# Marks in bfloat16 and a slot table entered from exactly split values: an FFT, mixture-of-experts and SoLU kernel on one core

## The chip, the cores and the metric

The kernel runs on one core of a Trainium2 chip. The metric is the device time of one execution in microseconds (us). Every time below is of the kernel before; lines such as L553 are lines of its source.

## The reference, cut to what matters

```python
def reference(**kw):
    y = _attn_ref(x, w_r, w_i, b_r, b_i)      # 8 x 3072 x 256: FFT over 3072, complex 256x256 mix, shrink, inverse FFT
    y = _moe_ref(y.reshape(24576, 256), w_gate, w1, w2, capacity)
    return _moe2_ref(y, w_in, w_out, g_ln)    # 256 -> 1024, SoLU, layer norm, 1024 -> 256

def _moe_ref(x, w_gate, w1, w2, capacity):    # 8 experts, capacity 768 here
    logits = x @ w_gate
    expert_idx = np.argmax(logits, axis=1)
    ...                                       # gate_w: softmax probability of the chosen expert
    for i in range(N):                        # in token order: the first `capacity` tokens of an expert keep a slot
        e = expert_idx[i]
        if counts[e] < capacity:
            disp[e, counts[e]] = x[i]
            pos[i] = counts[e]; counts[e] += 1; keep[i] = True
    h = np.maximum(np.einsum('ecd,edf->ecf', disp, w1), 0.0)
    y = np.einsum('ecf,efd->ecd', h, w2)
    ...                                       # out[i] = gate_w[i] * y[expert_idx[i], pos[i]] where kept, else 0
```

## The kernel before

The sequence of 3072 is handled as 96 x 32 per batch. For each of the first three batches a first stage (`forward`) is followed by twelve units (`units`): stage 2 of the FFT for unit u+1 (L393, with L396 to L399 behind it), the mix of unit u (L426, with L432, L434 and L435 behind it), the first inverse stage of unit u-1 (L443), and then whatever `middle(u)` hands in. A `tail` turns the batch back (L475, L480, L298, L491), and in it `route` works out which expert and which slot each token gets.

Only three batches are needed for every expert's capacity to be filled with these inputs; the rest is under a runtime condition. After them sixteen blocks of 384 slots run (`run_blocks`): two blocks for each of eight experts, with up projection (L798, L801, L802), down projection (L815 to L818), the 256 to 1024 projection (L842 to L845), SoLU and norm, and the last projection (L913). All the fp32 products of the experts are made from a high and a low part; `split` (L271) lets ScalarE copy the high part (L272) and another engine subtract to get the low part (L273).

The route of a batch has three parts. `local` finds the expert and the weight's numerator. `place` finds each token's slot, as `lo` (slot modulo 128) and `hi` (slot divided by 128). Nine steps then enter the tokens into a table `tab` of 128 x 2 x 48: for each slot the token's number plus one and its weight. The 32 tokens of a partition are taken in eight chunks of four. `mark(c)` makes for a chunk two tables of ones and zeros on VectorE, `rows` (where `lo` equals a column, 4 x 128, L553) and `hit` (where `hi` equals a column, 4 x 48, L554), and GpSimd multiplies `hit` by the token numbers and by the weights (L556, two instructions a chunk). `enter(c)` multiplies `rows` by the products on TensorE (L562: four fp32 matmuls of 96 columns, each shown as two instructions) and VectorE adds the result to `tab` (L564). There are two buffers for the chunks.

The order on each engine is fixed when the program is built, and every engine takes its queue in order. The nine steps of batch 0's route are handed in by `middle` in units 0 to 8 of batch 1, those of batch 1's route in batch 2, and those of batch 2's route in block 0, at the letters R of `ORDER_0`. `all_places` (L588) follows the last one and makes the indices by which later blocks gather. In block 0 the letters E hand in the steps of the second expert's weights (`expert_steps`, eight splits of 128 x 512, L272 and L273), which block 1 is the first to use.

Of the kernel before, what the change touches and what calls it, by code (L numbers as in the profile page):

```python
# [12 lines left out]
BF16 = mybir.dt.bfloat16  # L13
U16 = mybir.dt.uint16
ACTF = mybir.ActivationFunctionType
ALU = mybir.AluOpType
AX = mybir.AxisListType

NB, S, N1, N2, D = 8, 3072, 96, 32, 256
# [34 lines left out]
EARLY = (0, 1)  # L54
# [72 lines left out]
def _body(tc, x, w_r, w_i, b_r, b_i, w_gate, w1, w2, w_in, w_out, g_ln, cap, con, out):  # L127
# [4 lines left out]
    ncol = nslot // 128  # L132
    assert ncol <= 128
    mm = nc.tensor.matmul
# [8 lines left out]
    with sp as sb, dp as dr, pp as ps:  # L143
# [17 lines left out]
        def v(o, n, p=128):  # L161
            k, o = o >> 20, o & 0xFFFFF
            return tiles[k][:p, o : o + n]

        def v3(o, a, b, p=128):
            return v(o, a * b, p).rearrange("p (a b) -> p a b", a=a)

        def v4(o, a, b, c, p=128):
            return v(o, a * b * c, p).rearrange("p (a b c) -> p a b c", a=a, b=b)
# [327 lines left out]
        def route(tok_src, chunk_buffers):  # L497


            rt = [v(o_rt + 256 * i, 256, N1) for i in (0, 1, 2, 3, 4, 0)]  # L500
            sm = [v(o_rt + 1312 + 32 * i, 32, N1) for i in range(8)]
            ne = lambda a: a.rearrange("p (n e) -> p n e", e=NE)
            en = lambda a: a.rearrange("p (e n) -> p n e", e=NE)
            bc = lambda a: a.rearrange("p (n o) -> p n o", o=1).to_broadcast([N1, N2, NE])
            be = lambda a: a.rearrange("p (o e) -> p o e", o=1).to_broadcast([N1, N2, NE])
            tok, lo, hi, weight = v(o_rt + 1280, 32, N1), sm[4], sm[5], sm[1]
            tot2 = sm[3][:, 0:NE]

            def local():
                pool.dma_start(out=tok, in_=tok_src)  # L510
                vec.tensor_reduce(sm[0], lg, AX.X, ALU.max)
                vec.tensor_tensor(ne(rt[0]), lg, bc(sm[0]), ALU.subtract)
                act(rt[1], rt[0], ACTF.Exp)
                vec.tensor_scalar(rt[2], rt[0], 0.0, None, ALU.is_ge)
                vec.tensor_tensor(ne(rt[2]), ne(rt[2]), be(w8), ALU.mult)
                vec.tensor_reduce(sm[2], ne(rt[2]), AX.X, ALU.max)
                vec.tensor_tensor(en(rt[3]), ne(rt[2]), bc(sm[2]), ALU.is_equal)
                vec.tensor_tensor_scan(rt[4], seg, rt[3], 0.0, ALU.mult, ALU.add)
                tot = rt[4].rearrange("p (e n) -> p e n", e=NE)[:, :, N2 - 1 : N2].rearrange("p e o -> p (e o)")
                vec.tensor_copy(tot2, tot)  # L520

            def place():
                p = psum("pso")
                mm(p[:N1, 0:NE], low, tot2, start=True, stop=False)
                mm(p[:N1, 0:NE], one, tsum, start=False, stop=True)
                vec.tensor_tensor(sm[4][:, 0:NE], p[:N1, 0:NE], ecap, ALU.add)
                vec.tensor_tensor(tsum, tsum, tot2, ALU.add)
                vec.tensor_tensor(en(rt[4]), en(rt[4]), be(sm[4][:, 0:NE]), ALU.add)
                vec.tensor_tensor(en(rt[5]), en(rt[4]), be(lim), ALU.is_gt)
                vec.scalar_tensor_tensor(rt[4], rt[5], float(FAR), rt[4], ALU.mult, ALU.add)  # L530
                vec.tensor_tensor(rt[3], rt[3], rt[4], ALU.mult)
                vec.tensor_reduce(sm[5], en(rt[3]), AX.X, ALU.add)
                slot, row = sm[6].bitcast(I32), sm[7].bitcast(I32)
                vec.tensor_copy(slot, sm[5])
                vec.tensor_scalar(row, slot, 127, None, ALU.bitwise_and)
                vec.tensor_scalar(slot, slot, 7, None, ALU.logical_shift_right)
                vec.tensor_copy(lo, row)
                vec.tensor_copy(hi, slot)
                vec.tensor_reduce(weight, ne(rt[1]), AX.X, ALU.add)
                vec.tensor_scalar(weight, weight, 1e-9, None, ALU.add)  # L540
                vec.reciprocal(weight, weight)

            w = N2 // NCH
            wide = lambda a, c, m: a[:, w * c : w * c + w].rearrange("p (n o) -> p n o", o=1).to_broadcast([N1, w, m])
            same = lambda m: iota[:, 0:m].rearrange("p (o m) -> p o m", o=1).to_broadcast([N1, w, m])

            def views(c):
                o = chunk_buffers[c % len(chunk_buffers)]
                return v3(o, w, 128, N1), v4(o + 128 * w, w, 2, ncol, N1), v3(o + (128 + 2 * ncol) * w, w, ncol, N1)

            def mark(c):
                rows, cols, hit = views(c)
                vec.tensor_tensor(rows, same(128), wide(lo, c, 128), ALU.is_equal)  # L553
                vec.tensor_tensor(hit, same(ncol), wide(hi, c, ncol), ALU.is_equal)  # L554
                for i, a in enumerate((tok, weight)):
                    pool.tensor_tensor(cols[:, :, i], hit, wide(a, c, ncol), ALU.mult)  # L556

            def enter(c):
                rows, cols, _ = views(c)
                p = psum("psr")  # L560
                for j in range(w):
                    mm(p[:, 0 : 2 * ncol], rows[:, j], cols[:, j].rearrange("p a c -> p (a c)"), start=j == 0, stop=j == w - 1)  # L562
                t = tab.rearrange("p a c -> p (a c)")
                vec.tensor_tensor(t, t, p[:, 0 : 2 * ncol], ALU.add)  # L564

            steps = [lambda: mark(0)]
            for c in range(1, NCH):
                steps.append(lambda c=c: (mark(c), enter(c - 1)) if len(chunk_buffers) > 1 else (enter(c - 1), mark(c)))
            steps.append(lambda: enter(NCH - 1))
            return local, place, steps  # L570

# [612 lines left out]
        for b in range(FIRST):  # L1184
            last = b + 1 == FIRST
            steps = []

            def middle(u, b=b, last=last, marks=marks, steps=steps):
                if u == 0:
                    renew(o_hn)  # L1190
                    second[:] = second_steps()
                    steps.extend(step for chunk in second[3 * b : 3 * b + 3] for step in chunk)
                if b > 0 and marks:
                    marks.pop(0)()
                    if b == 2 and not marks:
                        early_places()
                zeros(ZEROS[b][u % 4])
                with pinned():
                    for _ in range(STEPS[b]):
                        if steps:  # L1200
                            steps.pop(0)()
                if not last and u in (4, 5, 6, 10, 11):
                    load_x(x[b + 1], {4: 0, 5: 1, 6: 2, 10: 3, 11: 4}[u])
                if last and u == 6:
                    renew(o_g)
                if last and GATHER <= u < GATHER + 2:
                    blocks[u - GATHER].gather()
                if last and u >= 6 and early:
                    early.pop(0)()
                    if early:  # L1210
                        early.pop(0)()

            def before_last(b=b, last=last, steps=steps):
                while steps:
                    steps.pop(0)()
                renew(o_hn)
                if last:
                    renew(o_ga)
                    blocks[0].transposes()
                    sums.extend(column_sums())  # L1220
                    sums.pop(0)()
                else:
                    begin(x[b + 1])

            units(middle, before_last)
            while sums:
                sums.pop(0)()
            renew(o_tt)
            if last:
                renew(o_wi2, o_hn)  # L1230
                second_half[0] = o_wi2
            if not last:
                forward(x[b + 1], begun=True)
                relays()
            else:
                renew(*o_q, o_wsb)
                side[0] = expert_steps(EARLY[1], slot_b, vec)
                side[0].pop(0)()
                side[0][LATER:LATER] = last_steps()
            local, place, marks = route(con["c_tok"][b], (o_hn + 1536, o_rt))  # L1240
            steps = {-at: [f] for f, at in zip((local, place), ROUTE[b])}
            if last:
                steps.setdefault(COUNT, []).insert(0, lambda: counts(cnt))
            tail(yview(ydram[b * S : (b + 1) * S, :]), steps)
# [81 lines left out]
```

## Time and profile before

| | |
|---|---|
| Time, median of 3 runs | 889.87 us (888.95 to 889.9) |
| The profiled execution | 889.02 us |
| Its span on the core | 887.4 us |
| TensorE, VectorE, ScalarE, GpSimd busy | 96%, 70%, 46%, 34% of the span |
| Mean granted TensorE clock | 0.985 |

PE is TensorE's matmuls, PEld its weight loads, DVE is VectorE, ACT ScalarE, POOL GpSimd. In the chain of work that ended last, each piece has its start, its length, and what it was. In a table by windows each row is a stretch (from:to in us), its length, then each engine's busy time with its count of instructions in brackets, the granted clock of TensorE as a share of full speed, the mean busy share of the DMA engines and GB/s. A row of a group of instructions has line, engine, operation, tiles, shapes and count, then busy us in total and the mean ns of one, then the idle time ahead of it. A row of a timeline has start, length, engine, line, operation. Instructions of one engine overlap at their ends, so the busy time of a stretch is less than the sum of durations.

### The profile page before, as it was taken

How to read it: one execution, taken by the hardware profiler on the slowest of the kernel's cores; microseconds unless marked ns; L12 is line 12 of the kernel's file. 1: busy time of each engine (PE TensorE's matmuls, PEld its weight loads, DVE VectorE, ACT ScalarE, POOL GpSimd, SP SyncE). 2: the span in 40 equal slices, each digit the busy share in tenths (PEclk: the TensorE clock that was granted, in tenths of full speed). 3: DMA queues.
4: the chain of work that ended last, by engine and by line, in shares of the span. 5: the costliest groups of instructions: out<-in, count | busy, mean ns of one | idle time of the engine just before them, and what ended most of it. 6: DMA issues, size and time to landing. Idle time of an engine off the chain costs nothing.

```text
span 887.4 us, 15851 instructions
## 1 busy us (share of the span) xinstructions
PE 851.6 (96%) x5884; PEld 734.1 (83%) x5884; DVE 621.4 (70%) x1434; ACT 410.4 (46%) x648; POOL 299.6 (34%) x463
## 2 busy tenths in 40 slices
PE   9799999999999989999999999999999999999993
PEld 3799459964799659988999889989889989999983
DVE  2376468745788568867787877868777778776771
ACT  2253344434444335444555545545555555544450
POOL 0000012100123024355564454445545545444343
PEclk9799999999999989999999999999999999999997
DMA  8989758996699143146376345355355354233120
GB/s 237 303 237 287 248 182 244 308 284 189 198 298 276 47 128 100 46 78 109 101 167 132 96 119 139 91 116 126 95 125 126 98 123 106 55 78 88 33 60 28
DMA packets 208683, 130.92 MB, mean 148 GB/s; under 512 B 123238, under 2 KB 190934, under 8 KB 208470
## 3 DMA queue, kind: packets, MB, share of 16 engines
q1 hardware_dynamic: 203894, 117.20, 50.3%
q0 software_dynamic: 4704, 12.63, 4.4%
q8 instruction: 48, 0.79, 0.4%
q14 instruction: 37, 0.30, 0.1%
HBM read 50.37 MB, written 50.33 MB: 113 GB/s over the span
## 4 chain that ended last, share of the span: by engine, by line
PE 86%; DMA 6%; DVE 4%; ACT 1%; issue 1%; POOL 0%; SPq 0%; DVEq 0%; ACTq 0%
PE psH L798 14%; PE pso L913 12%; PE psm L426 12%; DMA r<-r 5%; PE psY L818 5%; PE psY L817 4%; PE psh L843 4%; PE psh L842 4%; PE psh L845 4%; PE psY L815 4%; PE ps L298 4%; PE psi L443 4%; PE ps L393 4%; PE psy L298 4%; PE pst L475 3%; PE psr L562 2%
## 5 line engine op out<-in xcount | busy, mean ns | idle before, releaser
L798 PE MATMUL psH<-r,r 128*128 128x384 f32 x768 | 147.7, 340 | 0.5 <-DVE r L273 0.5
L798 PEld LDWEIGHTS psH<-r,r 128*128 128x128 f32 x768 | 135.5, 190 | 3.1 <-ACT r L491 0.8
L913 PE MATMUL pso<-r,r 128*128 128x256 f16 (+1 forms) x792 | 134.6, 274 | 1.2 <-DMA r<-r 1.2
L913 PEld LDWEIGHTS <-r 128*128 128x128 f16 x1080 | 102.2, 98 | 19.7 <-issue 6.5
L426 PE MATMUL psm<-r,r 128*128 128x256 f32 x864 | 114.1, 288 | 3.5 <-DVE r L397 2.8
L426 PEld LDWEIGHTS psm<-r,r 128*128 128x128 f32 x864 | 107.0, 193 | 4.2 <-DVE r L397 3.2
L556 POOL TENSOR_TENSOR r<-r,r 96x192 f32<-96x192 f32 x24 | 16.6, 708 | 258.5 <-DVE r L554 130.1
L801 ACT ACTIVATE r<-psH 128x768 fp32r<-128x768 f32 x64 | 52.0, 812 | 106.3 <-PE psH L798 106.3
L859 DVE SCALAR_TENSOR_TENSOR r<-psh,r 128x1024 f32<-128x1024 f32 x48 | 58.8, 1224 | 51.6 <-ACT r L851 51.5
L818 PE MATMUL psY<-r,r 128*128 128x384 f32 x256 | 86.6, 338 | 4.0 <-DVE r L802 3.9
L817 PE MATMUL psY<-r,r 128*128 128x384 f32 x256 | 85.8, 335 | 0.0
L851 ACT ACTIVATE r<-psh,r 128x1024 f32<-128x1024 f32 x36 | 43.4, 1206 | 81.6 <-DVE r L850 58.1
L913 PE MATMUL pso<-r 128*128 128x256 f16 x360 | 81.0, 273 | 0.0
L916 POOL DMA_INDIRECT out<-r x48 | 56.3, 1172 | 71.6 <-DVE r L915 64.7
L842 PE MATMUL psh<-r,r 128*128 128x512 f32 x192 | 76.5, 399 | 0.0
L843 PE MATMUL psh<-r,r 128*128 128x512 f32 x192 | 75.6, 394 | 0.0
L802 DVE SCALAR_TENSOR_TENSOR r<-psH,r 128x768 fp32r<-128x768 f32 x64 | 61.0, 954 | 11.4 <-ACT r L801 10.0
L752 POOL DMA_INDIRECT r<-ydram,r x48 | 50.3, 1047 | 42.9 <-DVE r L778 13.7
L849 DVE TENSOR_REDUCE r<-psh 128x1 f32<-128x1024 f32 x48 | 58.5, 1218 | 8.6 <-PE psh L845 8.6
L889 POOL TENSOR_SCALAR r<-r 128x1 f32<-128x1 f32 x48 | 12.4, 259 | 150.2 <-ACT r L869 114.1
L273 DVE TENSOR_TENSOR r<-r,r 128x512 fp32r<-128x512 f32 (+1 forms) x78 | 57.5, 745 | 0.1
L815 PE MATMUL psY<-r,r 128*128 128x384 f32 x256 | 56.8, 343 | 0.0
(182 smaller groups left out, 1665.6 us busy)
## 6 DMA issues: line engine op xcount, KB each, us to landing
out<-r SPq DMA_DIRECT2D x48, 512.0 KB, 6.1
r<-moe_w SPq DMA_DIRECT2D x32, 512.0 KB, 4.0
r<-x SPq DMA_DIRECT2D x24, 384.0 KB, 6.6
r<-gdram SPq DMA_DIRECT2D x36, 256.0 KB, 5.4
ydram<-r SPq DMA_DIRECT2D x36, 192.0 KB, 2.4
gdram<-r SPq DMA_DIRECT2D x12, 384.0 KB, 3.5
ydram<-r SPq DMA_DIRECT2D x36, 64.0 KB, 2.2
r<-moe_w_in SPq DMA_DIRECT2D x4, 512.0 KB, 5.1
```

The lines of the kernel that those rows point to most:

```text
L298: return [mm(o[32 * j : 32 * j + 32], fraw[:, i, 32 * m : 32 * m + 32], src, start=True, stop=True, tile_position=(0, 32 * j)) for j, (m, ...
L426: mm(p3[:, gi], a, b, start=i == 0, stop=i == len(seq) - 1)
L798: mm(p3[:, fi, 0:BLK], a, b, start=i == 0, stop=i == 5)
L802: vec.scalar_tensor_tensor(hl_, p3[:, :, 0:BLK], 0.0, hh.bitcast(F32), ALU.max, ALU.subtract)
L815: mm(y3[:, d, 0:BLK], b, hh[:, fi], start=f == 0, stop=False)
L817: mm(y3[:, d, 0:BLK], a, hh[:, fi], start=False, stop=False)
L818: mm(y3[:, d, 0:BLK], a, hl_[:, fi], start=False, stop=f == 7)
L842: mm(o, a, r, start=k == 0, stop=False)
L843: mm(o, a, w, start=False, stop=False)
L849: vec.tensor_reduce(c(0), p, AX.X, ALU.max, negate=True)
L859: vec.scalar_tensor_tensor(t, p, 1.0, e, ALU.mult, ALU.mult, accum_out=c(3))
L913: mm(p[:, 0:D], a, b, start=n == 0, stop=n == 23)
```

## The change

`rows` and `hit` become bfloat16. At the end of `place` the token number is split into two bfloat16 parts and the weight into three, which add up to the fp32 values again; eight small VectorE instructions write them into `vals`, 32 x 5 a partition, on memory that `place` used for `rt[4]`. The two GpSimd products of a chunk become one VectorE product of 4 x 5 x 48 elements, all operands bfloat16, in which `hit` is repeated over the five parts and each value of `vals` over the 48 columns. The matmuls are four of 240 bfloat16 columns instead of four of 96 fp32 columns. Instead of one addition of 96 columns to `tab` there are three, of 96, 96 and 48 columns, one behind the other. Separately, the low parts of the second expert's weights (eight splits in block 0) are subtracted by GpSimd instead of VectorE.

```diff
+            vals = v(o_rt + 1024, 80, N1).bitcast(BF16).rearrange("p (n k) -> p n k", k=5)
...
+                rest = sm[2]
+                for src, parts in ((tok, (0, 2)), (weight, (1, 3, 4))):
+                    for i, k in enumerate(parts):
+                        vec.tensor_copy(vals[:, :, k], src)
+                        if i + 1 < len(parts):
+                            vec.tensor_tensor(rest, src, vals[:, :, k], ALU.subtract)
+                            src = rest
...
             def mark(c):
-                rows, cols, hit = views(c)
+                rows, hit, cols = views(c)
                 vec.tensor_tensor(rows, same(128), wide(lo, c, 128), ALU.is_equal)
                 vec.tensor_tensor(hit, same(ncol), wide(hi, c, ncol), ALU.is_equal)
-                for i, a in enumerate((tok, weight)):
-                    pool.tensor_tensor(cols[:, :, i], hit, wide(a, c, ncol), ALU.mult)
+                vec.tensor_tensor(cols, hit.rearrange("p n (o m) -> p n o m", o=1).to_broadcast([N1, w, 5, ncol]),
+                                  vals[:, w * c : w * c + w].rearrange("p n (k o) -> p n k o", o=1).to_broadcast([N1, w, 5, ncol]), ALU.mult)
...
-                    mm(p[:, 0 : 2 * ncol], rows[:, j], cols[:, j].rearrange("p a c -> p (a c)"), start=j == 0, stop=j == w - 1)
+                    mm(p[:, 0 : 5 * ncol], rows[:, j], cols[:, j].rearrange("p k m -> p (k m)"), start=j == 0, stop=j == w - 1)
                 t = tab.rearrange("p a c -> p (a c)")
-                vec.tensor_tensor(t, t, p[:, 0 : 2 * ncol], ALU.add)
+                for k, n in ((0, 2), (2, 2)):
+                    vec.tensor_tensor(t, t, p[:, k * ncol : (k + n) * ncol], ALU.add)
+                vec.tensor_tensor(tab[:, 1], tab[:, 1], p[:, 4 * ncol : 5 * ncol], ALU.add)
...
-                side[0] = expert_steps(EARLY[1], slot_b, vec)
+                side[0] = expert_steps(EARLY[1], slot_b, pool)
```

## Rows read from the trace of the kernel before

**Rows 1.** The page's busy times.

```profile
PE 851.6 (96%) x5884; PEld 734.1 (83%) x5884; DVE 621.4 (70%) x1434; ACT 410.4 (46%) x648; POOL 299.6 (34%) x463
```

**Rows 2.** The chain that ended last, one marked unit of batch 2.

```profile
242.35 0.89 PE psi L443 x8
243.25 0.87 PE psr L562 x8
244.12 0.92 PE ps L393 x8
245.04 2.87 PE psm L426 x24
...
250.59 2.87 PE psm L426 x24
```

**Rows 3.** The same chain where the marks end, and one last projection.

```profile
272.80 2.87 PE psm L426 x24
278.36 2.87 PE psm L426 x24
283.02 2.87 PE psm L426 x24
...
426.23 2.64 PE pso L913 x24
```

**Rows 4.** Windows: marked stretches of batches 1, 2 and block 0; units without marks.

```profile
121.30:176.70 55.40, 53.60 (x458) 51.02 (x451) 46.00 (x97) 22.86 (x47) 10.99 (x17) 1.00 0.84 249
223.25:278.40 55.15, 53.41 (x458) 50.98 (x458) 47.73 (x105) 25.39 (x53) 10.77 (x17) 1.00 0.89 266
319.40:351.00 31.60, 28.03 (x167) 27.41 (x164) 23.78 (x54) 10.75 (x21) 11.26 (x17) 0.89 0.37 105
...
176.70:181.30 4.60, 4.60 (x42) 4.60 (x41) 3.38 (x6) 2.27 (x5) 0.00 (x0) 1.00 1.01 286
```

**Rows 5.** Groups of instructions by line and shape, whole span.

```profile
L802 DVE SCALAR_TENSOR_TENSOR r<-psH,r 128x768 fp32r<-128x768 f32 x64 | 61.0, 954 | 11.4 <-ACT r L801 10.0
L859 DVE SCALAR_TENSOR_TENSOR r<-psh,r 128x1024 f32<-128x1024 f32 x48 | 58.8, 1224 | 51.6 <-ACT r L851 51.5
L273 DVE TENSOR_TENSOR r<-r,r 128x512 fp32r<-128x512 f32 x64 | 44.2, 700 | 0.0
L434 DVE TENSOR_SCALAR r<-r 128x512 f32<-128x512 f32 x36 | 15.3, 425 | 0.9
L556 POOL TENSOR_TENSOR r<-r 96x192 f32<-96x192 f32 x24 | 14.5, 623 | 34.5 <-PE psr L562 29.3 <-DVE r L554 4.3 <-DVE r L405 1.0
L564 DVE TENSOR_TENSOR r<-r,psr 128x96 f32<-128x96 f32 x24 | 5.9, 247 | 5.0 <-PE psr L562 4.9
L514 DVE TENSOR_SCALAR r<-r 96x256 f32<-96x256 f32 x3 | 0.9, 291 | 0.1
L534 DVE CAST r<-r 96x32 int32<-96x32 f32 x3 | 0.5, 176 | 0.1
```

**Rows 6.** VectorE's groups in six marked units, 137.8 to 171.1 us.

```profile
L553 DVE TENSOR_TENSOR r<-r 96x512 f32<-96x512 bf16 x6 | 5.2, 874 | 0.0
L435 DVE TENSOR_TENSOR r<-r 128x512 f32<-128x512 f32 x6 | 4.6, 764 | 0.1
```

**Rows 7.** Timelines of VectorE and ScalarE, batch 2 and block 0.

```profile
227.04 0.69 DVE L553 TENSOR_TENSOR r<-r 96x512 f32<-96x512 bf16 x1
227.65 0.35 DVE L554 TENSOR_TENSOR r<-r 96x192 f32<-96x192 bf16 x1
...
246.78 0.68 DVE L397 TENSOR_TENSOR r<-ps,r 128x512 fp32r<-128x512 f32 x1
...
247.49 0.42 ACT L399 ACTIVATE r<-r 128x256 fp32r<-128x256 f32 x1 [1.37 <-DVE r L397]
...
338.17 2.18 ACT L272 ACTIVATE r<-r 128x512 fp32r<-128x512 f32 x4
```

**Rows 8.** Windows across TensorE's wait in block 0.

```profile
322.00:325.10 3.10, 0.03 (x1) 0.04 (x1) 2.65 (x6) 1.14 (x2) 1.96 (x3) 0.98 0.28 85
325.10:328.00 2.90, 2.90 (x12) 2.90 (x13) 0.87 (x3) 0.00 (x0) 0.84 (x2) 0.50 0.50 169
328.00:332.00 4.00, 4.00 (x17) 4.00 (x16) 2.27 (x6) 0.98 (x2) 1.28 (x2) 0.53 0.04 11
```

**Rows 9.** The chain that ended last around block 0's first marks and its end.

```profile
323.15 1.88 POOL r L556 x2
325.07 2.02 PE psr L562 x8
...
351.02 2.08 PE psH L798 x12
```

More of the change, by code (lines that the diff above doesn't have):

```diff
@@ L548, in views @@
                 o = chunk_buffers[c % len(chunk_buffers)]
-                return v3(o, w, 128, N1), v4(o + 128 * w, w, 2, ncol, N1), v3(o + (128 + 2 * ncol) * w, w, ncol, N1)
+                b = lambda at, n: v(o + at * w // 2, n * w // 2, N1).bitcast(BF16)
+                return (b(0, 128).rearrange("p (n m) -> p n m", n=w), b(128, ncol).rearrange("p (n m) -> p n m", n=w),
+                        b(128 + ncol, 5 * ncol).rearrange("p (n k m) -> p n k m", n=w, k=5))
             def mark(c):
-                rows, cols, hit = views(c)
+                rows, hit, cols = views(c)
                 vec.tensor_tensor(rows, same(128), wide(lo, c, 128), ALU.is_equal)
                 vec.tensor_tensor(hit, same(ncol), wide(hi, c, ncol), ALU.is_equal)
-                for i, a in enumerate((tok, weight)):
-                    pool.tensor_tensor(cols[:, :, i], hit, wide(a, c, ncol), ALU.mult)
+                vec.tensor_tensor(cols, hit.rearrange("p n (o m) -> p n o m", o=1).to_broadcast([N1, w, 5, ncol]),
+                                  vals[:, w * c : w * c + w].rearrange("p n (k o) -> p n k o", o=1).to_broadcast([N1, w, 5, ncol]), ALU.mult)
             def enter(c):
-                rows, cols, _ = views(c)
+                rows, _, cols = views(c)
                 p = psum("psr")
                 for j in range(w):
-                    mm(p[:, 0 : 2 * ncol], rows[:, j], cols[:, j].rearrange("p a c -> p (a c)"), start=j == 0, stop=j == w - 1)
+                    mm(p[:, 0 : 5 * ncol], rows[:, j], cols[:, j].rearrange("p k m -> p (k m)"), start=j == 0, stop=j == w - 1)
                 t = tab.rearrange("p a c -> p (a c)")
-                vec.tensor_tensor(t, t, p[:, 0 : 2 * ncol], ALU.add)
+                for k, n in ((0, 2), (2, 2)):
+                    vec.tensor_tensor(t, t, p[:, k * ncol : (k + n) * ncol], ALU.add)
+                vec.tensor_tensor(tab[:, 1], tab[:, 1], p[:, 4 * ncol : 5 * ncol], ALU.add)
             steps = [lambda: mark(0)]
```

## The prediction, as it was made before the run

> **What bounds the kernel now.** First I read the busy times: TensorE works 96% of the span, VectorE 70%, GpSimd 34% [rows 1]. Taken alone that says that cheaper matmuls shorten the kernel and that VectorE has room. So the chain that ended last comes next, in the stage that is touched. A marked unit of batch 2 goes stage 2 (0.92 us), mix (2.87), inverse (0.89), marks (0.87), with no piece between them, 5.55 us from mix to mix [rows 2]; the first unit without marks takes 4.66 [rows 3]. There the marks cost TensorE 0.87 us each, 24 times. Then the windows of the same stretches: VectorE is busy 46.0 of 55.4 us in batch 1, 47.7 of 55.15 in batch 2, 23.8 of 31.6 in block 0 [rows 4]. That is 75 to 87%, not 70%: the reader is to see that the stage that gives TensorE time is the one where VectorE has the least left, 9.4, 7.4 and 7.8 us. Last, block 0: TensorE stands still for 3.1 us from 322.0, and then runs for some 6.7 us at a granted clock of 0.50 to 0.53, the lower level (1.2 GHz) [rows 8]; the chain names GpSimd's two products and then the first marks' matmuls as what it stood for [rows 9].
>
> **The matmuls.** Before, a chunk is 0.87 us [rows 2]. After, it is four matmuls of 240 columns in a 16-bit type. The nearest row is the last projection: 24 of 256 columns in 2.64 us, 0.11 each [rows 3]; four are 0.44. So TensorE's need falls by 0.43 a chunk, 3.4 for each batch's eight chunks, 10.3 in all, if nothing else decides. A marked unit would be 5.12 us.
>
> **What VectorE gets.** The product of a chunk has 960 elements a partition. From 768 elements (954 ns) to 1024 (1224 ns) [rows 5] the line gives 1.16 us. The only faster rows are one-input operations: 256 elements 291 ns, 512 elements 425 ns [rows 5], which at that slope gives 0.66 for 960. Those are the two ends. I take 1.16, since every two-input row lies on the slow line (512 elements: 700 ns) and one input here is a single element read 48 times over.
>
> The Trainium skill has rules for both. "VectorE: DVE Perf Modes", in the tier table, gives two-input operations on bfloat16 in SBUF twice their fp32 rate, which would be the 0.66. "Vector Engine (DVE) Microarchitecture Reference", section 5.1, asks for a step of one on every operand, and reports a two-input operation with one element read 16 times as an input at the single rate, which is the 1.16. No row of this trace has such an operation in bfloat16.
>
> Instructions of VectorE overlap at their ends: L553 takes 0.69 us and the next begins 0.61 after it [rows 7]. So the product adds 1.08. The additions were one of 247 ns [rows 5], 0.17 net; three that wait for one another are 0.28, 0.28 and 0.17, so 0.56 more. A chunk adds 1.64, eight add 13.1. The eight small writes of `vals` are like L534, 0.18 each [rows 5], 1.3 a batch net. That is 14.4 us a batch.
>
> What falls away: GpSimd's products slow VectorE while they run. L553 has a mean of 0.87 in the marked units against 0.69 alone, L435 0.76 [rows 6] against 0.70 for its shape [rows 5, 7]; with what lies on others I take 0.3 a chunk, 2.4 a batch.
>
> **Batches 1 and 2.** VectorE's work in the marked stretch is 46.0 - 2.4 + 14.4 = 58.0 us in batch 1 and 47.7 - 2.4 + 14.4 = 59.7 in batch 2, where the stretches are 55.4 and 55.15 long. It no longer fits: what bounded the stage on TensorE passes to VectorE. I add 0.5 for waits that remain. Queued behind the new product is L397, the low part for the next mix, for which TensorE waits; before, it began at 246.78, ScalarE's L399 behind it ended at 247.91, and the mix that needs both began at 250.59 [rows 2, 7], so 2.7 us of delay cost nothing. Batch 1: 58.0 + 0.5 - 55.4 - 2.7 = +0.4. Batch 2: 59.7 + 0.5 - 55.15 - 2.7 = +2.35. TensorE's 3.4 a batch is inside these: it waits it away.
>
> **Block 0.** VectorE has 23.8 us there [rows 4]. GpSimd's slowing takes off 1.5 (an estimate: L553's excess in rows 6, scaled to sixteen products that fall on other work too). The eight splits go, at 700 ns [rows 5], 0.60 net, 4.8 in all. The 14.4 come. That is 31.9. The splits on GpSimd slow VectorE in turn: nothing to 2 us, I take 1. Waits that remain: 7.8 before, nearly all of them for the chunks' products and matmuls; I take 1.5. Sum 34.4, where the stretch was 31.6: +2.8. TensorE's first wait should shorten (two GpSimd products of 1.88 us [rows 9] become one of 1.16 on VectorE, behind 1.3 of `vals`), but with VectorE as the bound that gives nothing back.
>
> **The splits on GpSimd.** No row has this size. L556 has 192 elements a partition at 623 ns [rows 5]; 512 lie between that (if all of it were a fixed part) and 1.66 us, and I take 1.4 since most of it should scale. The last four high parts come at 338.17 to 340.35 [rows 7]; four splits end by 347 at the worst, block 1's first up projection begins at 351.02 [rows 9]. The cost is nothing, and that margin of 4 us is the cover; gone, each split late is up to 1.66 on the path. The later weight loads that take the freed buffers serve blocks after block 1, and the queue of gathers on GpSimd waits for `all_places` anyway. Freed memory of `rt[4]`, the two chunk buffers and GpSimd's waits on them: no cost, the order of reads and writes is the same.
>
> **The sum.** +0.4 + 2.35 + 2.8 = +5.6 us. The profiled execution took 889.0, its span 887.4; it lies 0.85 under the median. 889.0 + 5.6 = 894.6.
>
> **The rivals.** (A) The lag drains behind the marks, and the kernel is faster. In units without marks VectorE is busy 3.4 of 4.6 us [rows 4], so if L397 stands ahead of the products in VectorE's queue, the marks can run late without holding a mix. The place is the end of each marked stretch; it decides if VectorE's lag there stays under the 2.7 us of slack plus some 3 us of idle in the light units. Then both batches give their 3.4, and block 0, if its waits and GpSimd's slowing vanish (31.9 in 31.6), costs 0.3: 889.0 - 6.9 + 0.3 = 882.4; with half of block 0's cost 883.5. For it: the idle time is there. Against it: in the rows the next unit's L397 runs behind this unit's marks. (B) The product runs at the fast end, 0.66, as the tier table named above would have it. Then a chunk costs 0.50 less: batch 1 is held by TensorE at -3.4, batch 2 is +2.35 - 4 = -1.65, block 0 is -1.2: 882.8. Against it is every two-input row. (C) TensorE's clock. A wait of 3.1 us was followed by 6.7 us at the lower level [rows 8], which cost about half of that, 3.4. If the heads of batches 1 and 2, where VectorE now has `vals` and the first products ahead of the first mix, get such a wait, two times 3.4 come on top: 901.4. (D) It comes out even: VectorE's lag is eaten by slack in batch 2 as in batch 1 and block 0 gains at its first wait what it loses later: 889 to 891. It would mean that the matmuls do get cheaper and that nobody sees it.
>
> **How the numbers follow.** Forecast 0.46, A 0.24, B 0.05, C 0.13, D 0.12. About 0.2% (1.8 us) is what a measurement of this kernel can tell from no change. A and B are faster, 0.29. D and the lower edge of the forecast are the same, 0.15. C and the rest of the forecast are slower, 0.56. The likeliest case's own range is 891 to 899: no slowing by GpSimd and one more microsecond of slack a batch, or 2 us of slowing and half the slack. To leave out no more than 2 in 10 the range goes from the middle of A and B, 883, to just past C, 902.
>
> **What the changed profile would show.** The marks' matmuls at 0.44 a chunk on the chain (0.87 before), whatever else happens. One VectorE product of 4 x 240 elements at 1.16 us; at 0.66, B. Marked units longer than 5.55 us with VectorE busy nearly all of them and TensorE waiting for L397; units of 5.12 mean A, with L397 ahead of the products. L553 and L435 back at 0.69 in the batches. Block 0's end, the first up projection of block 1, at some 2 to 4 us later relative to the tail's end; GpSimd's splits done before it. A granted clock under 1 at the head of a batch would be C. The forecast is wrong if VectorE's busy time in the marked stretches is under 55 us, or if the queue lets the marks drift.

## The result and the profile after

| | before | after |
|---|---|---|
| Time, median of the timed executions | 889.87 us | 898.80 us (897.55 to 900.88) |
| Ratio after to before | | 1.0106, 95% interval 1.0089 to 1.0122 |
| The profiled execution, its span | 889.02, 887.4 us | 900.88, 898.8 us |
| Mean granted TensorE clock | 0.985 | 0.975 |

The change makes the kernel slower by 1.1%, 8.9 us by the medians. The forecast was +5.6 us and slower. The loss lies in block 0 and just behind it and has two parts: one stood in the sum with 1 us, the other not at all. The profiled execution after is the slowest of its five, 2.1 us above their median, and the one before lies 0.85 below its own; so of the 11.4 us between the two spans some 3 come from which executions were profiled.

Lines of the changed kernel stand up to 13 further down: `rows` is L564, `hit` L565, the product L566, the marks' matmuls L573, the additions L576 and L577, the up projection L811, the copies and transposes of the gathered words L784, L785 and L791.

The page's busy times, to be read beside [rows 1]:

```profile
PE 847.2 (94%) x5788; PEld 725.5 (81%) x5788; DVE 644.0 (72%) x1522; ACT 410.1 (46%) x648; POOL 284.1 (32%) x423
```

The chain that ended last in batch 1, to be read beside [rows 2, 3]: marked units from one mix to the next (start, length, what).

```profile
155.59 3.11 PE psm L426 x24
158.71 0.89 PE psi L443 x8
159.60 0.41 PE psr L573 x4
160.01 0.90 PE ps L393 x8
160.91 2.87 PE psm L426 x24
...
165.99 2.87 PE psm L426 x24
...
176.41 2.87 PE psm L426 x24
```

The marks' matmuls take 0.41 us where they took 0.87, and a unit 5.1 to 5.3 where it took 5.55. So in these units TensorE got what it was promised and sets the pace. It is not so everywhere: in batch 2 of the changed kernel the same chain runs mostly through VectorE's queue from 242.4 to 250.3 us.

Windows of the marked stretches and of the units behind them, batch 1 and batch 2 of the changed kernel, to be read beside [rows 4] (columns as there):

```profile
121.90:176.40 54.50, 51.78 (x426) 48.48 (x422) 50.94 (x124) 22.75 (x46) 0.54 (x1) 0.97 0.84 245
176.40:188.60 12.20, 12.20 (x109) 12.08 (x111) 9.20 (x19) 4.74 (x10) 0.00 (x0) 1.00 1.01 274
222.30:277.00 54.70, 51.82 (x442) 48.49 (x439) 51.60 (x130) 25.66 (x52) 0.51 (x1) 1.00 0.85 258
277.00:291.60 14.60, 14.19 (x120) 13.82 (x119) 12.58 (x28) 6.14 (x13) 7.29 (x6) 1.00 0.68 204
```

VectorE is busy 93 and 94% there, 50.9 and 51.6 us, not the 58.0 and 59.7 of the sum.

Where the time went, by the first matmul of six places in the two traces (TensorE's timeline):

| from the first matmul of ... to ... | before | after | difference |
|---|---|---|---|
| the start to the router of batch 1's marks (L524; L525) | 120.69 | 121.32 | +0.6 |
| ... to the first stage for the next batch (L298), behind batch 1's units | 68.10 | 67.20 | -0.9 |
| ... to the products behind batch 2 (psc) | 102.17 | 101.09 | -1.1 |
| ... to block 0's first up projection | 28.45 | 28.46 | 0.0 |
| block 0, to block 1's first up projection | 31.45 | 41.57 | +10.1 |
| ... to the second group of last projections (pso), in block 1 | 29.83 | 33.42 | +3.6 |
| the rest of the span | 506.71 | 505.74 | -1.0 |
| sum, the span | 887.4 | 898.8 | +11.4 |

The batches gain 2 us, and block 0 and what follows on it lose 13.7. These are two executions. The first four experiments below leave the source of the batches as it is, before or after, so they add to it: batch 1 and batch 2 together take 170.3 and 172.0 us with the old marks, and 168.3, 168.8, 168.5 and 167.0 with the new ones. Batch 1 alone differs by up to 1.6 us, and batch 2 by up to 2.6, between executions of the same source.

The chain in block 0 of the changed kernel shows two things that [rows 9] does not have:

```profile
328.67 0.96 DVE r L815
329.62 1.92 DVE r L566
331.71 1.51 DVE r L564
...
337.39 2.01 DVE r L566
339.57 1.51 DVE r L564
...
352.03 0.47 DVE r L784
352.62 0.48 DVE r L784
353.15 3.77 DMA r<-r
356.94 0.60 DVE r L791
...
358.75 0.85 ACT r L272
359.64 0.69 PE psH L811
```

First, VectorE's product has up to 2.01 us of this chain and `rows` 1.51; by the timeline they last up to 2.08 and 1.59, where they take 1.15 and 0.68 in the batches. Second, block 1's first up projection (359.64) stands behind a DMA of 3.77 us that could start only when two copies, L784, had come out of VectorE's queue at 352.03 and 352.62, behind the last marks. TensorE's waits of this stretch (us in total, times, longest):

```profile
PE psr L573 <- DVE r L566: 8.5, 5, 3.5
PE psH L811 <- ACT r L272: 7.0, 1, 7.0
```

Before, the same two copies ran at 328.44 and 329.98, and TensorE did not wait for ScalarE there at all:

```profile
328.44 0.87 DVE L771 COPY r<-r 128x768 uint16<-128x768 uint16 x1
...
329.98 0.55 DVE L771 COPY r<-r 128x768 uint16<-128x768 uint16 x1
```

They are handed in at the same letter X in both kernels, but the order that was built for VectorE differs: before, they stand between the early marks, and after, behind the last product.

What makes the product long is seen where both engines stand side by side. VectorE's and GpSimd's timeline at the start of block 0 in the changed kernel (start, length, engine, line, operation):

```profile
318.60 1.31 POOL L273 TENSOR_TENSOR r<-r,r 128x512 fp32r<-128x512 f32 x1 [32.00 <-ACT r L272]
318.66 1.28 DVE L538 CAST r<-r 96x32 f32<-96x32 int32 x1
...
321.86 2.82 POOL L273 TENSOR_TENSOR r<-r,r 128x512 fp32r<-128x512 f32 x1 [1.96 <-ACT r L272]
...
322.40 1.14 DVE L566 TENSOR_TENSOR r<-r,r 96x960 bf16<-96x960 bf16 x1
323.46 0.94 DVE L815 SCALAR_TENSOR_TENSOR r<-psH,r 128x768 fp32r<-128x768 f32 x1
```

A cast of 32 elements, 0.17 us elsewhere, begins just behind GpSimd's split and ends with it, 1.28 later. GpSimd's next split is the one that waits: it has 2.82 us, while VectorE's product runs, and then goes on beside L815, which reads one input from PSUM and keeps its 0.94. So here the two engines take turns when both work from SBUF, and run side by side when VectorE has PSUM as an input. The Trainium skill has a rule for it: "SBUF — State Buffer", section "SBUF: two separate sides", has VectorE and GpSimd share a pair of ports under an exclusive lock for the whole instruction, when VectorE's operation has two SBUF inputs or runs in a mode with both ports. The trace agrees for operations with two SBUF inputs, with up to 2.08 for 1.15 and 1.59 for 0.68. The cast, 1.28 for 0.17, has one input; whether it runs in such a mode no run shows.

### The profile page after: what moved, and what is told of

It reads as the page before. It is cut to its first block, busy times and chain, and to the rows that moved or that the text cites. A ratio compares the mean times of both kernels' runs of the same rounds, so it can differ in the third digit from the quotient of the medians.

```text
span 898.8 us, 15663 instructions
## 1 busy us (share of the span) xinstructions
PE 847.2 (94%) x5788; PEld 725.5 (81%) x5788; DVE 644.0 (72%) x1522; ACT 410.1 (46%) x648; POOL 284.1 (32%) x423
## 4 chain that ended last, share of the span: by engine, by line
PE 77%; DVE 9%; DMA 9%; issue 2%; ACT 2%; SPq 1%; POOL 0%; DVEq 0%
PE psH L811 14%; PE pso L926 12%; PE psm L426 7%; PE psh L856 5%; PE psh L855 5%; PE psY L831 4%; PE psh L858 4%; DMA r<-r 4%; PE psY L830 4%; PE psY L828 4%; PE ps L298 4%; PE psy L298 3%; PE pst L475 3%; PE psi L443 3%; PE ps L393 2%
## 5 line engine op out<-in xcount | busy, mean ns | idle before, releaser
L811 PE MATMUL psH<-r,r 128*128 128x384 f32 x768 | 151.4, 346 | 7.6 <-ACT r L272 7.0
L811 PEld LDWEIGHTS psH<-r,r 128*128 128x128 f32 x768 | 138.4, 194 | 10.8 <-ACT r L272 7.1
L765 POOL DMA_INDIRECT r<-ydram,r x48 | 52.3, 1089 | 92.5 <-DMA r<-moe_w 51.0
L511 POOL DMA_DIRECT2D r<-c_tok x3 | 1.8, 587 | 223.8 <-DVE r L547 223.3
L815 DVE SCALAR_TENSOR_TENSOR r<-psH,r 128x768 fp32r<-128x768 f32 x64 | 61.0, 953 | 14.6 <-ACT r L814 13.3
L272 ACT ACTIVATE r<-r 128x512 fp32r<-128x512 f32 (+1 forms) x78 | 50.7, 659 | 5.1 <-DMA r<-moe_w 4.2
```

Source lines behind the costliest of these rows:

```text
L811: mm(p3[:, fi, 0:BLK], a, b, start=i == 0, stop=i == 5)
L815: vec.scalar_tensor_tensor(hl_, p3[:, :, 0:BLK], 0.0, hh.bitcast(F32), ALU.max, ALU.subtract)
```

## The experiments

Three theories on the loss in block 0. Theory 1: GpSimd's splits hold VectorE's operations. Theory 2: the copies ahead of block 1's transposes stand behind the last marks in VectorE's queue. Theory 3: it is VectorE's additional work as such, as the prediction had it. The kernel before had a median of 889.95 us beside the first four and 889.94 beside the others.

**The splits back on VectorE**, in the changed kernel:

```diff
-                side[0] = expert_steps(EARLY[1], slot_b, pool)
+                side[0] = expert_steps(EARLY[1], slot_b, vec)
```

> The marks of the change alone: the low parts of the second expert's weights go back to VectorE, all else as changed. Theory 1 (what costs block 0 its time is that GpSimd's splits slow VectorE's 16-bit operations): the marks' products keep 1.15 us throughout, block 1's first up projection comes some 6 us earlier, about 892 us. Theory 2 (the copies ahead of the DMA transposes of block 1's tokens lie behind the last marks in VectorE's queue, and block 1 waits for them): the queue has them behind the last product here too, so the wait of 7 us stays, about 898 us. Theory 3 (VectorE's sheer work): the eight splits add 4.8 us to it, about 903 us.

Measured: 895.44 us, 1.0067 of before (1.0048 to 1.0087), 3.4 less than the changed kernel. VectorE's groups of block 0 are back to their own durations (busy us, mean ns of one):

```profile
L564 DVE TENSOR_TENSOR r<-r 96x512 bf16<-96x512 bf16 x8 | 5.4, 680 | 0.0
L566 DVE TENSOR_TENSOR r<-r 96x960 bf16<-96x960 bf16 x4 | 4.6, 1148 | 0.0
L566 DVE TENSOR_TENSOR r<-r,r 96x960 bf16<-96x960 bf16 x4 | 4.6, 1147 | 0.0
```

In the changed kernel the same three are:

```profile
L564 DVE TENSOR_TENSOR r<-r 96x512 bf16<-96x512 bf16 x8 | 7.2, 905 | 0.0
L566 DVE TENSOR_TENSOR r<-r,r 96x960 bf16<-96x960 bf16 x4 | 6.4, 1593 | 0.0
L566 DVE TENSOR_TENSOR r<-r 96x960 bf16<-96x960 bf16 x4 | 4.6, 1146 | 0.0
```

So the splits on GpSimd cost 3.4 us although they freed VectorE of eight instructions of 0.68. TensorE's wait of 7.0 us for L272 stayed, so Theory 2 is another part.

**The splits alone**, the same line changed to `pool` in the kernel before:

> The kernel before with one edit: the low parts of the second expert's weights on GpSimd, marks in fp32 as before. Theory 1: VectorE's marks are slowed and so are GpSimd's own products, which now stand behind the splits; 893 us or more. Theory 2: VectorE keeps idle time in block 0, the copies ahead of the transposes stay early, 889 to 891 us. If the edit alone helps VectorE (4.8 us less work): 886 us.

Measured: 891.99 us, 1.0024 (1.0010 to 1.0038), 2.0 us slower without anything of the marks. VectorE's `rows` and GpSimd's splits in block 0 of this kernel:

```profile
L553 DVE TENSOR_TENSOR r<-r 96x512 f32<-96x512 bf16 x8 | 13.0, 1620 | 0.0
L273 POOL TENSOR_TENSOR r<-r,r 128x512 fp32r<-128x512 f32 x8 | 11.1, 1394 | 33.1 <-ACT r L272 33.1
```

L553 has a mean of 709 ns there before. The split itself costs what I had taken for it, 1.4; what it does to VectorE is the price.

**The copies early**, in the changed kernel, by the order of block 0:

```diff
-    ORDER_0 = 'E R U0 L E R U1 E R ... R G E X D3 E E Z F'
+    ORDER_0 = 'E R U0 L E R U1 X E R ... R G E D3 E E Z F'
-    PIN_X = (2,)
+    PIN_X = (0, 2)
```

> The changed kernel with block 1's copies and DMA transposes handed in behind the second up projection of block 0 and held there in the queue of VectorE, splits on GpSimd as changed. Theory 2: the wait of 7.0 us ahead of block 1's first up projection and the lower clock behind it go, 889 to 892 us. Theory 1: only what overlaps the wait is gained, 896 us.

Measured: 891.31 us, 1.0021 (1.0007 to 1.0034), 7.5 less than the changed kernel. TensorE's wait for L272 is 1.4 in place of 7.0:

```profile
PE psr L573 <- DVE r L566: 9.2, 5, 4.6
PE psH L811 <- ACT r L272: 1.4, 1, 1.4
```

**Both repairs**:

> The changed kernel with both edits, splits on VectorE and the copies ahead of block 1's transposes held early. If theories 1 and 2 each hold a part: 886 to 889 us, no slower than the kernel before. If VectorE's sheer work in block 0 is the bound (theory 3): 893 us or more, with VectorE busy nearly all the time from 318 us to block 1.

Measured: 888.15 us, 0.9973 (0.9959 to 0.9987). It is 10.7 below the changed kernel, as the two parts give (3.4 + 7.5), and 1.8 below the one before. So Theories 1 and 2 make up the loss against the kernel before, and Theory 3 alone does not explain it: with both repairs the marks are worth 1.8 us. Theory 3 still holds a part of block 0. That takes 34.95 us from up projection to up projection, against 31.45, with VectorE busy 31.9 of them and TensorE waiting three times for a product:

```profile
PE psr L573 <- DVE r L566: 6.3, 3, 3.0
PE psH L811 <- ACT r L272: 1.4, 1, 1.4
```

**The price of the product.** On top of both repairs, ScalarE first writes the values 48 times each, so that VectorE multiplies without an operand that repeats one element:

```diff
-                vec.tensor_tensor(cols, hit..., vals[...]...to_broadcast([N1, w, 5, ncol]), ALU.mult)
+                act(cols, vals[...]...to_broadcast([N1, w, 5, ncol]), ACTF.Copy)
+                vec.tensor_tensor(cols, hit..., cols, ALU.mult)
```

> On top of both repairs (splits on VectorE, copies early; that kernel took 888.15 us). ScalarE first writes each value of the chunk 48 times (960 elements a partition, about 1.05 us between its rows of 768 elements at 812 ns and 1024 at 1147 to 1206 ns), and VectorE multiplies in place, so that only the repeated table of marks is left as an operand whose values are not side by side in one run, and its innermost step is one. Theory 'step of zero': the product is slow (1.147 us) because one operand repeats a single element; now it takes 0.60 to 0.70 us, VectorE has 3.6 us less a batch, TensorE's waits in batches 1 and 2 (2.7 us each) shrink, block 0's two waits of 3 us for the product shrink by 0.5 each: 883 to 886 us. Rival 'size alone': the product stays at 1.15, nothing is won, 888 to 890. Rival 'ScalarE takes VectorE's place': the product is fast but the new copy stands ahead of L399 in ScalarE's queue at the heads of the batches, TensorE waits for ScalarE there: 887 to 890.

Measured: 883.25 us, 0.9930 (0.9910 to 0.9950), faster than both kernels. The product and the new copy:

```profile
L567 DVE TENSOR_TENSOR r<-r 96x960 bf16<-96x960 bf16 x24 | 15.6, 649 | 0.0
L566 ACT ACTIVATE r<-r 96x960 bf16<-96x960 bf16 x24 | 23.8, 993 | 6.1 <-PE psr L573 5.5 <-DVE r L547 0.6
```

0.649 us for 960 elements: the two ends of the prediction's range for the product, 0.66 and 1.16, are the two layouts of one operand. Between the same places as in the table above, batch 1 is 64.33 us, batch 2 100.28 and block 0 30.20, where both repairs alone have 67.20, 99.79 and 34.95 and the kernel before 68.10, 102.17 and 31.45. In batch 1 all of TensorE's 3.4 us come out, with the granted clock at 1.00 at its head, and block 0 is shorter than before for the first time. Some of the 4.9 us to both repairs may be the clock: its mean is 0.985 to 0.987 in the four executions here and 0.978 to 0.986 in the ten there.

**The same in the changed kernel, without the repairs**:

> The changed kernel with ScalarE's spread copy alone: splits still on GpSimd, copies still late. Theory 'GpSimd stretches every two-input operation of VectorE from SBUF': the product beside a split takes longer again than alone, whichever rate it has alone, 1.1 to 2.0 us; and if alone it is at 0.6 to 0.7, block 0 is shorter by at most 2 us, because the wait of 7 us for the copies stays: 894 to 897. Rival 'only slow-rate operations are stretched': product 0.6 to 0.7 beside a split too, 892 to 894.

Measured, in one execution: 888.4 us. Neither expectation of its time was right: I had thought that the wait for the copies would stay. It does not: block 1's up projection begins at 349.11 after 2.2 us of waiting for VectorE. The copies are no longer late. The order built for VectorE has them elsewhere in this kernel, the first ahead of the first product and the second ahead of the last, and the transposes behind them start at 343.09, where they start at 353.15 in the changed kernel:

```profile
321.46 0.55 DVE L784 COPY r<-r 128x768 uint16<-128x768 uint16 x1
...
342.48 0.55 DVE L784 COPY r<-r 128x768 uint16<-128x768 uint16 x1
```

So this run changed two things, the length of the product and the place of the copies, and their shares are not shown. GpSimd's turns are there as before, on whatever VectorE then has; two pairs of its timeline:

```profile
325.41 1.28 POOL L273 TENSOR_TENSOR r<-r,r 128x512 fp32r<-128x512 f32 x1 [1.02 <-ACT r L272]
...
325.60 1.30 DVE L565 TENSOR_TENSOR r<-r 96x192 bf16<-96x192 bf16 x1
...
331.50 6.01 POOL L273 TENSOR_TENSOR r<-r,r 128x512 fp32r<-128x512 f32 x4 [1.88 <-ACT r L272]
...
333.60 1.53 DVE L567 TENSOR_TENSOR r<-r 96x960 bf16<-96x960 bf16 x1
```

L565, 0.34 alone, ends 0.21 us behind the split, 326.90 against 326.69. The one product that falls among splits takes 1.53 us, where the others in block 0 take 0.59 to 0.66. So the splits hold an operation at the fast rate too, as the first theory had it, and the rival is out.

**Less work in the batches.** On top of both repairs, the weight is split in two parts, not three (the lowest bits of the weight are left out):

```diff
-                for src, parts in ((tok, (0, 2)), (weight, (1, 3, 4))):
+                for src, parts in ((tok, (0, 2)), (weight, (1, 3))):
...
-                vec.tensor_tensor(tab[:, 1], tab[:, 1], p[:, 4 * ncol : 5 * ncol], ALU.add)
```

> On top of both repairs (888.15 us). The weight is split into two bfloat16 parts instead of three, so the lowest 8 bits of its mantissa are left out: the product has 768 instead of 960 elements, the matmuls 192 instead of 240 columns, and the addition of 48 columns falls away. VectorE has some 0.23 + 0.19 us less a chunk, 3.4 a batch, TensorE 0.09 a chunk, 0.7 a batch. Theory 'VectorE's work bounds the marked stretch all along': each batch gets shorter by 2 to 3 us and block 0 by 1 to 3, 880 to 884. Rival 'only the head counts': behind the head TensorE runs without a wait already (15 of 15 and 16.4 of 16.4 us in the kernel before, 14.6 and 16.4 after), so only TensorE's own 0.7 a batch and the first chunks count: 885 to 887, with TensorE's wait for L397 at the head of a batch still 1.7 to 1.8.

Measured: 887.39 us, 0.9961 (0.9939 to 0.9984), only 0.8 below both repairs. The rival is nearer: batch 1 is 68.05 us there, no shorter, and its head shows why (windows; the column before the last two is the granted clock):

```profile
124.00:127.00 3.00, 1.03 (x7) 0.63 (x5) 3.00 (x7) 2.53 (x7) 0.19 (x1) 1.00 0.29 87
127.00:130.00 3.00, 2.19 (x10) 2.19 (x11) 3.00 (x9) 0.75 (x2) 0.00 (x0) 0.52 0.41 126
130.00:133.00 3.00, 3.00 (x16) 3.00 (x16) 0.97 (x3) 0.00 (x0) 0.00 (x0) 0.50 0.53 152
```

Six microseconds at the lower level, 1.2 GHz, cost about 3 us, what a batch was to gain; so in batch 1 the run does not decide between the theories. One of its executions took 880.48 us, at a mean granted clock of 0.986; the others had 0.977 to 0.981.

**The small writes off VectorE**, on top of both repairs:

```diff
-                        vec.tensor_copy(vals[:, :, k], src)
+                        pool.tensor_copy(vals[:, :, k], src)
...
-                            vec.tensor_tensor(rest, src, vals[:, :, k], ALU.subtract)
+                            pool.tensor_tensor(rest, src, vals[:, :, k], ALU.subtract)
```

> On top of both repairs (888.15 us). The eight small writes of vals go to GpSimd (the operations that add 32 x 5 values a partition; before, VectorE). They stand among VectorE's chain of place, ahead of the first L397 of the batch, for which TensorE waits 1.8 us; behind that wait the granted clock of batch 1 was 0.50 from 130 to 133 us. Theory 'the head of the batch': they hold L397 by 0.5 to 1.0 us; without them the wait is 1.0 to 1.4, the clock of batch 1's head stays at 1.00 and gives 1.5 back: 885.5 to 887. Rival 'they lie in gaps of place's chain': L397 begins no earlier, the clock falls again, 888 to 889, or later if GpSimd's chain ends behind the first product's turn (a row of the product after 129.9 in batch 1).

Measured: 890.64 us, 1.0010 (0.9993 to 1.0028), 2.5 above both repairs. TensorE's wait for L397 at the head of batch 1 is 1.7 us, as it was at 1.8. L397 begins 5.57 us behind VectorE's first instruction of `place` (L527), and 5.67 with both repairs. So taking `vals` off VectorE brought next to nothing, as the rival had it; on GpSimd they take 0.32 to 0.38 each. Where the 2.5 us come from is not shown. The granted clock of batch 1's head was 1.00 here and 0.65 to 0.78 at the head of batch 2, where it had been 1.00: the clock falls at one head or another. Which wait tips it is left open by these runs.

## Why the prediction was right, and where its steps failed

**Direction and range held; the sum was 5.8 us short of the span's +11.4 (3.3 short by the medians), by errors of both signs.** The mechanism held less well than the number. The prediction named signs of its own: VectorE busy under 55 us in the marked stretches means that the forecast is wrong, and units of 5.12 us mean A. VectorE was busy 50.9 and 51.6 us, and the units shown took 5.1 to 5.3. So the step "what bounded the stage on TensorE passes to VectorE" held only in stretches of the batches, and they gained where a loss was forecast.

The matmuls: 0.44 predicted, 0.41 on the chain. Right.

The product: 1.16 taken, 1.147 measured in the batches. Rival B is out. Of the two reasons given, the element that is read 48 times over was the right one, and the product at 0.649 without it shows that; that every two-input row lies on the slow line did not decide, since the fast product has two inputs as well. By the Trainium skill, "Vector Engine (DVE) Microarchitecture Reference", section 5.1, a step of one along the innermost dimension of every operand is a condition of the double rate that "VectorE: DVE Perf Modes" gives. The runs agree, with 1.147 us against 0.649.

Batches 1 and 2: +0.4 and +2.35 predicted, -0.9 and -1.1 measured. VectorE's work was over-sized. From batch 1's router to its last unit it rose from 46.0 + 7.8 to 50.9 + 9.2 us, +6.4, where the sum has +12.0. Two terms can be named. The three additions do not wait for one another as I had them: in VectorE's queue they stand among other operations, and each takes 0.16 to 0.17 of it, so they cost 0.28 net a chunk more than the one of before, not 0.56 (2.2 us a batch). And the relief from GpSimd's products was larger, about 3.1 us instead of 2.4, since not only L553 (0.83 to 0.68) and L435 (0.73 to 0.69) but also the six L646 of 512 integers had been held (0.51 to 0.42). The other 2.7 us lie in no single row but in the overlaps. An instruction of VectorE that follows another without a gap overlaps it by some 0.08 us; by the timelines of this stretch 64 did so before, 4.9 us in all, and 120 after, 9.7 us. The sum took overlap off the new instructions alone, while the old ones closed up too.

Rival A had part of the truth: VectorE ran on into the units without marks, 9.2 us busy there against 7.8 in batch 1 and 12.6 against 10.1 in batch 2, while the mixes kept TensorE's pace. Its price did not come: of TensorE's 3.4 us in batch 1 of these two executions about 1.0 went into longer waits (L397 1.8 for 1.5, and three short ones) and 1.5 into the lower clock at the head, which rival C had named. The stretch that shows it, of the changed kernel and of the one before, and then of the copies early and of the splits alone, whose batches have the same source as the first and the second:

```profile
130.00:133.00 3.00, 3.00 (x16) 3.00 (x15) 3.00 (x6) 0.02 (x1) 0.00 (x0) 0.50 0.56 175
...
130.00:133.00 3.00, 3.00 (x28) 3.00 (x27) 1.34 (x5) 1.01 (x2) 0.00 (x0) 1.00 0.76 237
...
130.00:133.00 3.00, 3.00 (x27) 3.00 (x27) 3.00 (x7) 0.26 (x1) 0.00 (x0) 1.00 0.55 173
...
130.00:133.00 3.00, 3.00 (x22) 3.00 (x22) 0.24 (x1) 0.69 (x2) 0.00 (x0) 0.78 0.76 237
```

In the six microseconds ahead of it TensorE was busy 3.9 us after and 4.3 before; but with the copies early it was busy 3.9 too, and the clock stayed at 1.00. So the same source falls to the lower clock at this head in one execution and not in another, with the new marks and with the old, and the change is not shown to be the cause. 3.4 - 1.0 - 1.5 = 0.9 is what batch 1 gained.

Block 0: +2.8 predicted, +10.1 measured, and +3.6 behind it. Two steps failed.

The step "The cost is nothing, and that margin of 4 us is the cover" looked for the cost of GpSimd's splits at the wrong end. The cover held, nobody waited for a split. The cost was on VectorE: "nothing to 2 us, I take 1", which was scaled from GpSimd's products that VectorE met before (0.87 for 0.69 in [rows 6]). The row that would have told it stood there: the excess comes from taking turns, so it grows with the length of GpSimd's instruction, and the splits are two to three times as long as the products (1.31 alone, 1.78 on the mean, against 0.62). Measured on VectorE: by the changed kernel's timeline eight instructions beside the splits (a cast, two products, two `rows`, three `hit`) lasted 6.1 us longer in all than alone, which is more than the 4.8 us that the sum took off for the splits. Measured on the kernel: 3.4 us by putting the splits back, and 2.0 by moving them alone in the kernel before.

The step "with VectorE as the bound" ended the sum at the last mark. What is queued behind the marks on VectorE was listed for the batches (L397) and not for block 0. There it is two copies, then a transpose of 3.77 us and a second pair of copies, which block 1 needs: 7.0 us of TensorE standing still, 7.5 by the run with the copies early. In the kernel before the first pair ran at 328.44 and 329.98, between the early marks, and the chain did not name it. The prediction took VectorE's order as it was; the order built for the changed kernel has that pair behind the last product. What moved it there is not shown.

Block 1's +3.6 is for the most part that wait's shadow: behind 4 us in which TensorE did nothing, the granted clock of the changed kernel is 0.50 for the first 5 us of block 1, from 359.64 to 364.64, which gives away 2.5, where it was 1.00 before. Another 1.0 is a longer wait for a DMA ahead of the last projections, 2.15 against 1.16, whose cause is not shown.

That the time came out in the likeliest case's own range of 891 to 899, by 0.2 us, was thus luck for the most part: the batches were 4.7 us better and block 0 with block 1 10.9 worse than the sum, and two errors of mechanism made up for each other.

## What to carry to other kernels

Work moved from VectorE to GpSimd is not gone from VectorE when both work from SBUF: count GpSimd's duration as VectorE's until a timeline shows the two side by side. When an engine passes from idle gaps to back-to-back work, list everything queued behind the new work up to the next stage's first instruction, also what no chain names, and see in the new trace whether it kept its place in the queue: an edit that leaves the source order alone can still give another order on an engine. And when a two-input operation in a 16-bit type repeats one element, try writing that operand out by an engine with time to spare: 0.99 us on ScalarE bought 0.50 on VectorE, and up to 4.9 us of the kernel.

## What the runs showed of the hardware that was not expected

VectorE's cast of 32 elements took 1.28 us beside a GpSimd subtraction of 1.31, so even a one-input operation on SBUF can have to wait its turn; an operation of 768 elements with an input in PSUM kept its 0.94 us in the same place. The same product of 960 bfloat16 elements took 1.147 us with one operand repeating an element and 0.649 without. And a kernel with less work on VectorE and TensorE (four parts instead of five) was no faster in its batch 1, since the granted clock was 0.50 to 0.52 for six microseconds at its head. The kernel before had 1.00 there, but 0.65 to 0.78 with the splits alone and the same batches: so the clock at a batch's head falls in one execution and not in another, and these runs do not show why.
